# Where the stacked weights are made, when groups are rounded, and where tile 0's first layer stands in a routed mixture-of-experts kernel

## The chip, the cores and the metric

The kernel runs on one core of a Trainium2 chip, as one program from the inputs to the output. The metric is the device time in microseconds (us). Beside it stands one profiled execution, whose trace has every instruction of the five engines (TensorE or PE, with its weight loads as PEld; VectorE or DVE; ScalarE or ACT; GpSimd or POOL; SyncE or SP, which issues most transfers) with start, length and what ended the idle time before it.

## The reference

Three stages stand one behind the other. `x` is 4 sequences of 5,696 tokens of 128 numbers, so N = 22,784 tokens.

```
y  = irfft(rfft(x, 2S) * rfft(h, 2S))[:S]          # a long convolution, per channel
# soft experts: 8 experts of 4 slots each, D = 128, F = 1024
logits = y @ phi                                   # N x 32
slots  = softmax over tokens(logits).T @ y         # 32 x 128
out_s  = relu(slots @ w1[e]) @ w2[e]               # per expert e
z  = softmax over slots(logits) @ out_s            # N x 128
# routed experts: one of 8 per token
gate = z @ w_gate + modality_bias[modality_id]     # N x 8
e    = argmax(gate);  g = softmax(gate)[e]
out  = g * (relu(z @ v1[e]) @ v2[e])               # v1, v2: moe2_w1, moe2_w2
```

Each token's z is a weighted sum of 32 slot outputs. So the kernel never forms z: a token is carried as its 32 softmax weights, and `out_s` is multiplied into the experts' first layer once, which gives a stacked weight of 32 rows per expert. The same is done with the gate's weights.

## The kernel before

**Up to the slots** the program convolves by Fourier transforms on TensorE, makes the slot logits, the softmax weights and the slots' inputs, and loads the slot experts' weights. `prefetch` (line 1528) then issues four loads of the routed experts' first layer, two experts each, into the tile `mw` (called A in the trace). `slot_experts` computes the slots' outputs `oT`. All of this is untouched.

**The part that the change touches first** is written out by hand in `build` (lines 1569 to 1639): on each engine the instructions run in the order in which the program text issues them.

- `gate_weights` multiplies the slots' outputs with the gate's weights. `gate(i)` (function `gate_logits`) makes the logits of the i-th quarter of the tokens: matmuls `gl`, a ScalarE copy (L743, L746), transposes `psl`, and later `add` on VectorE (L764), which adds the modality's bias `bf`. `base` fills `bf` with the first modality's bias, `other` overwrites it where a token has the second (L541). `warm(n)` issues n matmuls whose result nobody reads.
- `push(eh, hf)` calls `expert_stack`: four experts (`eh` is 0 or 1) and half of their columns (`hf`). TensorE multiplies `oT` with `mw` (L781, tile e), ScalarE rounds the product (L782), and the returned function, called later through `seconds(i)`, makes the remainder on VectorE (L785). With the second half of a group of four experts it also issues eight stores of the stacked weights into DRAM (`s_w`, L790).
- `ro.choose` picks the expert of each token of the first part (26 groups of 128 tokens): VectorE's maximum, difference and comparison, ScalarE's exponential (L888), and a one-hot matrix (L894) that is written over the memory of the logits. `ro.offsets` counts tokens per expert with two matmuls (`pre`) and a chain of small VectorE instructions; `ro.gates`, `ro.positions` and `ro.masks` follow.
- `ro.prep(n)` prepares n pairs of groups for sorting: VectorE forms m (L1008), a one-hot of positions (L1010) and token numbers (L1012); then `hi` rounds m on ScalarE (L1016) and `lo` makes the remainder on VectorE (L1019). `prep_all` runs all three. `ro.sort(n, put)` sorts a pair by matmuls `srt` (L1035), copies it on ScalarE (L1037) and scatters it with an indirect transfer from POOL into DRAM (`s_rec`, L1153).
- `ro.table` makes the table of tiles: which expert and which rows of `s_rec` a tile of 256 tokens has. SP reads its entries (`entry`).

**The routed experts** (`routed_experts`) go over 89 tiles. For tile k, `load_w` loads the expert's weights in up to two transfers, `load_rec` the sorted records, `tokT` transposes them (tile pst), `l1(k, h)` makes half h of the first layer (matmuls L1302; ScalarE's rounded relu L1304; VectorE's remainder L1305), `l2` the second layer, `out1` and `out2` the output, `store` scatters it. In between, the rest of the tokens is routed: `late` is a list of small steps (choice, offsets, preparation, tables of the later parts), `run_late(n)` does n of them, and `spend(us)` does as many as a written-down cost allows. `run(k0, k1)` writes out the order; before the loop over tiles it has a prologue, which the change touches. A tile's records may be loaded once the groups of its chunk are scattered: tile 0 needs 9 pairs of groups, tiles 1 and 2 need 11, tile 3 needs 13. Nine pairs are sorted in `build`, four more in the prologue.

Of the kernel before, what the change touches and what calls it, by code (L numbers as in the profile page):

```python
# [53 lines left out]
W3 = 5  # L54
W4 = 8
W5 = 2
W6 = 3
W7 = 10
YBUF = 16
FAR = 1 << 20  # L60
# [1127 lines left out]
def routed_experts(nc, tc, R, P, out, ro, tabs, put):  # L1188

    ident = P["ident"]  # L1190
    with tc.tile_pool(name="p6", bufs=1, reuse_waits="tile") as sp, tc.tile_pool(name="p6p", bufs=1, space=PS, reuse_waits="tile") as pp:
# [155 lines left out]
        def run(k0, k1):  # L1347
# [7 lines left out]
            go(load_rec, k0)  # L1355
            go(load_w, k0, second_layer)
            if k0 == 0:
                for _ in range(2):
                    prep_all(2)
                    ro.sort(2, put)  # L1360
                run_late(7)
            go(entry, k0 + 1)
            go(load_w, k0 + 1, first_layer)
            go(entry, k0 + 2)
# [1 line left out]
            go(load_rec, k0 + 2)  # L1366
            go(load_w, k0 + 1, second_layer)
            go(load_w, k0 + 2, first_layer)
            go(load_rec, k0 + 3)
            go(load_w, k0 + 2, second_layer)  # L1370
            go(tokT, k0)
            go(l1, k0, 0)
            go(l1, k0, 1)
            if k0 == 0:
                spend(PRE)
            go(tokT, k0 + 1)
            for k in range(k0, k1):
# [79 lines left out]
def build(nc, tc, I, O, dbg=None):  # L1457
# [13 lines left out]
    with tc.tile_pool(name="const", bufs=1) as cp:  # L1471
# [98 lines left out]
        with tc.manual_schedule():  # L1570
            base, other = fill
            g = 4 * PIECES[0][1]
            base(bf, 0, g)
            other(bf, 0, g)
            nc.gpsimd.memset(pad, 0.0)
            nc.sync.dma_start(R["rec"][SPARE * TM:].rearrange("(p j) c -> p (j c)", p=128), pad)
            ro = Routing(nc, P, rt, rq, rc, slices(a2, 10 * F), pp, c, l2, pat, ex, v, tabs)
            ro.number()
            put = scatters(nc, tc, R, ro)
            nc.gpsimd.tensor_copy(P["identr"], P["ident"])  # L1580

            def gate(i, between=None):
                return gate_logits(nc, xr, pp, P, cT, bd, bf, l2, i, between)
            def stack(eh, hf):
                return expert_stack(nc, pp, R, oT, mw, mh2, ml2, eh, hf)

            def warm(n):
                keep_warm(nc, pp, P["ones"], n, tag="l", bufs=2)
            stacks, adds = [], []

            def push(eh, hf):
                stacks.append(stack(eh, hf))

            def seconds(*i):

                for i in i:
                    stacks[i]()
                    yield us(512)

            def sums(*i):  # L1600

                for i in i:
                    adds[i]()
                    yield us(400)

            warm(W5)
            gate_weights(nc, pp, oT, wg, bd)
            warm(W5)
            base(bf, g, NG)
            add = gate(0, lambda: warm(W6))  # L1610
            other(bf, g, NG)
            add()
            adds.append(gate(1))
            choose = ro.choose(PARTS[0])
            run_all(itertools.islice(choose, 4))
            push(0, 0)
            run_all(choose)
            offsets = ro.offsets(PARTS[0])
            next(offsets)
            push(0, 1)  # L1620
            push(1, 0)
            run_all(offsets, ro.gates(*PARTS[0][:2]), ro.positions(*PARTS[0][:2]), ro.masks(*PARTS[0][:2]))
            ro.prep_all(1)
            run_all(seconds(0))
            ro.sort(1, put)
            ro.prep_all(2)
            run_all(seconds(1))
            push(1, 1)
            ro.sort(2, put)
            for i in range(3):  # L1630
                ro.prep_all(2)
                if i == 1:
                    run_all(seconds(2, 3))
                ro.sort(2, put)
            run_all(ro.table(tabs[0], CP[1]))
            run_all(sums(0))
            adds.append(gate(2))
            adds.append(gate(3))
            run_all(sums(1, 2))
        if dbg:  # L1640
            nc.sync.dma_start(O["l2"], l2)
            nc.sync.dma_start(O["tab"], tabs[2])
# [30 lines left out]
```

## Time and profile before

| | us |
|---|---|
| three runs | 984.76, 980.85, 983.04 |
| their median | 983.04 |
| the profiled execution | 979.97 |
| its span, first to last instruction | 977.9 |

Shares of the span in which an engine was busy: TensorE 91%, its weight loads 83%, VectorE 71%, ScalarE 62%, POOL 52%. The mean granted TensorE clock was 0.969 of 2.4 GHz.

How to read the profile: a row of the timeline has the start and length of an instruction (or of several merged ones, x4), its engine, line and operation, what it writes and reads, and in brackets how long the engine had been idle before it and what ended that. A product of two fp32 matrices shows as two matmul instructions. A transfer's row on SP is its issue, not its landing.

### The profile page before, as it was taken

The page shows a single profiled execution, that of the slowest core. Times are in us where ns is not written, and L with a number is a line of the kernel's source. Part 1 is how long each engine was busy: PE and PEld are TensorE (multiplying, and loading weights), DVE is VectorE, ACT ScalarE, POOL GpSimd, SP SyncE. Part 2 cuts the span into 40 slices and gives each one's busy share as a digit, 9 for nine tenths or more (in the row PEclk, how much of TensorE's full clock was granted, in tenths as well). Part 3 has the DMA queues.
Part 4 walks back from the last instruction along what each step waited for, and adds up shares of the span by engine and source line. Part 5 has one row for each costly group of instructions (what it writes and reads, how often), then busy time and mean ns, then how long its engine had stood idle before and what let it go on. Part 6 is the DMA issues. An engine that isn't in the chain of part 4 may idle for free. (4 is left out here: it accounts for less than half of the span.)

```text
span 977.9 us, 22643 instructions
## 1 busy us (share of the span) xinstructions
PE 894.0 (91%) x7552; PEld 814.6 (83%) x7552; DVE 695.1 (71%) x1451; ACT 603.2 (62%) x1104; POOL 513.0 (52%) x619
## 2 busy tenths in 40 slices
PE   7999999999999999899845689989999999999996
PEld 7898888878888899788514689979999998999995
DVE  1658687777777555893486779979889987775553
ACT  2655585674765656752233467767777777776673
POOL 2215756738657825381231266656657666665443
PEclk9999999999999999999956899999999999999998
DMA  9915857748559866899966222222223323322221
GB/s 137 329 48 145 264 158 221 239 148 256 191 170 284 327 231 206 331 407 382 303 169 217 73 60 74 75 62 72 71 69 78 76 76 82 75 73 69 59 64 39
DMA packets 147396, 156.66 MB, mean 160 GB/s; under 512 B 71341, under 2 KB 124493, under 8 KB 145210
## 3 DMA queue, kind: packets, MB, share of 16 engines
q1 hardware_dynamic: 137306, 137.43, 47.5%
q0 software_dynamic: 9968, 17.71, 5.6%
q8 instruction: 63, 1.03, 0.5%
q14 instruction: 59, 0.48, 0.2%
HBM read 227.40 MB, written 63.70 MB: 298 GB/s over the span
## 5 line engine op out<-in xcount | busy, mean ns | idle before, releaser
L1305 DVE SCALAR_TENSOR_TENSOR hl<-ph,hh 128x1024 fp32r<-128x1024 f32 x178 | 217.3, 1222 | 92.8 <-ACT hh L1304 91.5
L1342 POOL DMA_INDIRECT out<-y,ids x178 | 180.6, 1015 | 104.4 <-ACT y L1330 54.8
L1304 ACT ACTIVATE hh<-ph 128x1024 fp32r<-128x1024 f32 x178 | 182.7, 1027 | 57.4 <-PE ph L1302 50.1
L1317 PE MATMUL acc<-hh,w 128*128 128x256 f32 x712 | 214.9, 302 | 0.0
L1318 PE MATMUL acc<-hl,w 128*128 128x256 f32 x712 | 201.3, 283 | 0.0
L1319 PE MATMUL acc<-hh,w 128*128 128x256 f32 x712 | 201.3, 283 | 0.0
L1318 PEld LDWEIGHTS acc<-hl,w 128*128 128x128 f32 x712 | 136.5, 192 | 0.0
L1319 PEld LDWEIGHTS acc<-hh,w 128*128 128x128 f32 x712 | 136.1, 191 | 0.0
L1317 PEld LDWEIGHTS acc<-hh,w 128*128 128x128 f32 x712 | 135.9, 191 | 0.0
L1153 POOL DMA_INDIRECT s_rec<-so,dst x80 | 76.9, 962 | 97.4 <-ACT so L1037 85.8
L205 PEld LDWEIGHTS psx<-G,A 128*128 128x128 f32 x890 | 111.7, 196 | 19.1 <-DVE V L217 11.7
L205 PE MATMUL psx<-G,A 128*128 128x128 f32 x890 | 121.6, 284 | 2.5 <-DVE A L140 1.3
L130 PE MATMUL psa<-fw,xs 128*128 128x180 f32 x640 | 110.0, 325 | 11.2 <-POOL xs L169 5.0
L1302 PE MATMUL ph<-x,w 128*128 128x256 f32 x712 | 116.2, 286 | 4.1 <-DVE hl L1305 3.2
L130 PEld LDWEIGHTS psa<-fw,xs 128*128 128x128 f32 x640 | 99.5, 198 | 23.2 <-POOL xs L169 12.6
L140 DVE COPY A<-psa 64x360 f32<-64x360 f32 x160 | 88.5, 553 | 31.6 <-PE psa L130 28.0
L134 ACT COPY A<-psa 64x360 f32<-64x360 f32 x160 | 84.1, 526 | 37.4 <-PE psa L130 34.4
L1302 PEld LDWEIGHTS ph<-x,w 128*128 128x128 f32 x712 | 98.7, 193 | 5.0 <-issue 4.0
L218 POOL TENSOR_TENSOR Y<-Y,V 128x256 f32<-128x256 f32 (+1 forms) x92 | 66.4, 722 | 58.3 <-DVE V L217 49.8
L169 POOL COPY xs<-xr 89x512 f32<-89x512 f32 x68 | 45.7, 674 | 89.6 <-PE psa L130 73.1
L229 ACT COPY yt<-psy 128x512 f32<-128x512 f32 (+1 forms) x92 | 52.7, 572 | 64.9 <-PE psy L102 40.5
L216 DVE TENSOR_TENSOR Y<-psx,H 128x512 f32<-128x512 f32 (+1 forms) x92 | 61.9, 673 | 35.4 <-PE psx L205 32.0
(245 smaller groups left out, 1525.4 us busy)
## 6 DMA issues: line engine op xcount, KB each, us to landing
w<-s_w SPq DMA_DIRECT2D x86, 1536.0 KB
s_yt<-yt SPq DMA_DIRECT2D x88, 256.0 KB
xr<-x SPq DMA_DIRECT2D x16, 640.0 KB
xr<-s_yt SPq DMA_DIRECT2D x18, 512.0 KB
s_w<-ws SPq DMA_DIRECT2D x32, 256.0 KB
L<-s_yt SPq DMA_DIRECT2D x16, 512.0 KB
rt<-s_rec SPq DMA_DIRECT2D x89, 66.0 KB
rt<-s_rec SPq DMA_DIRECT2D x89, 64.0 KB
```

The lines of the kernel that those rows point to most:

```text
L130: nc.tensor.matmul(ps[:, i, :4 * NPAIR], x, fw1, start=True, stop=True)
L134: i = nc.scalar.copy(o, v)
L140: i = nc.vector.tensor_copy(o, v)
L205: nc.tensor.matmul(ps[:, m, :], A[:, 2 * i + m // 2, :, m % 2], G[:, 4 * i + m, :], start=True, stop=True)
L1153: d = nc.gpsimd.indirect_dma_start(rows, bass.IndirectOffsetOnAxis(ap=ro.dst[:LANES, i:i + 1], axis=0), o, None, bounds_check=SPARE * TB - ...
L1302: nc.tensor.matmul(ps[:, TM * j:TM * j + TM], w[k % 3][:, f:f + 128], x[k], start=True, stop=True)
L1304: nc.scalar.activation(o, ps, AF.Relu)
L1305: nc.vector.scalar_tensor_tensor(hl[:, 4 * h:4 * h + 4].rearrange("p j t -> p (j t)"), ps, 0.0, o.bitcast(F32), op0=ALU.max, op1=ALU.subtract)
L1317: nc.tensor.matmul(acc[k], wh, hh[:, f], start=(f == 0), stop=False)
L1318: nc.tensor.matmul(acc[k], wh, hl[:, f], start=False, stop=False)
L1319: nc.tensor.matmul(acc[k], wl, hh[:, f], start=False, stop=(f == 7))
L1342: i = nc.gpsimd.indirect_dma_start(out, bass.IndirectOffsetOnAxis(ap=d[:, j:j + 1], axis=0), y[:, j, :], None, bounds_check=NT - 1, oob_is ...
```

## The change

Three moves, all of them in the order of issue. The work itself stays the same, but for five warm-up matmuls that are dropped.

1. In `build`, `push` for all four (eh, hf) is issued around the first two quarters' logits: two ahead of `gate(0)`, the third between the matmuls and the copy of `gate(0)`, the fourth behind `gate(1)`. The remainders (`seconds`, now `low`) follow early as well: two ahead of the first `add`, the third behind the choice, the fourth in the first preparation; with them go the stores. `base` for the later tokens now stands behind the first two products, `other` for them behind the table.
2. In the five preparations of `build`, `hi` of the next groups is issued ahead of `ro.sort` of the groups before, and `lo` behind it.
3. In the prologue of `run`, tile 0's `tokT` and `l1` stand behind the first two sorted pairs instead of behind all four; the second preparation and sort, the load of tile 3's records, and the seven late steps follow behind them.

```diff
@@ run, the prologue
             if k0 == 0:
-                for _ in range(2):
-                    prep_all(2)
-                    ro.sort(2, put)
-                run_late(7)
+                prep_all(2)
+                ro.sort(2, put)
             go(entry, k0 + 1)
             go(load_w, k0 + 1, first_layer)
...
             go(load_w, k0 + 2, first_layer)
-            go(load_rec, k0 + 3)
-            go(load_w, k0 + 2, second_layer)
             go(tokT, k0)
             go(l1, k0, 0)
             go(l1, k0, 1)
             if k0 == 0:
+                prep_all(2)
+                ro.sort(2, put)
+            go(load_rec, k0 + 3)
+            go(load_w, k0 + 2, second_layer)
+            if k0 == 0:
+                run_late(7)
                 spend(PRE)
             go(tokT, k0 + 1)
@@ build
-            def push(eh, hf):
-                stacks.append(stack(eh, hf))
-
-            def seconds(*i):
-
+            def push(*which):
+                for w in which:
+                    stacks.append(stack(*w))
+
+            def low(*i):
                 for i in i:
                     stacks[i]()
-                    yield us(512)
...
+            first, cols = PARTS[0], PARTS[0][:2]
             warm(W5)
             gate_weights(nc, pp, oT, wg, bd)
-            warm(W5)
+            push((0, 0), (0, 1))
             base(bf, g, NG)
-            add = gate(0, lambda: warm(W6))
-            other(bf, g, NG)
+            add = gate(0, lambda: push((1, 0)))
+            low(0, 1)
             add()
             adds.append(gate(1))
-            choose = ro.choose(PARTS[0])
-            run_all(itertools.islice(choose, 4))
-            push(0, 0)
-            run_all(choose)
-            offsets = ro.offsets(PARTS[0])
-            next(offsets)
-            push(0, 1)
-            push(1, 0)
-            run_all(offsets, ro.gates(*PARTS[0][:2]), ro.positions(*PARTS[0][:2]), ro.masks(*PARTS[0][:2]))
-            ro.prep_all(1)
-            run_all(seconds(0))
-            ro.sort(1, put)
-            ro.prep_all(2)
-            run_all(seconds(1))
-            push(1, 1)
-            ro.sort(2, put)
-            for i in range(3):
-                ro.prep_all(2)
-                if i == 1:
-                    run_all(seconds(2, 3))
-                ro.sort(2, put)
+            push((1, 1))
+            run_all(ro.choose(first))
+            offsets = ro.offsets(first)
+            low(2)
+            run_all(offsets, ro.gates(*cols), ro.positions(*cols), ro.masks(*cols))
+            todo = 0
+            for i, n in enumerate((1, 2, 2, 2, 2)):
+                hi, lo = ro.prep(n)
+                hi()
+                if todo:
+                    ro.sort(todo, put)
+                lo()
+                if i == 0:
+                    low(3)
+                todo = n
+            ro.sort(todo, put)
             run_all(ro.table(tabs[0], CP[1]))
-            run_all(sums(0))
+            other(bf, g, NG)
+            sums(0)
             adds.append(gate(2))
             adds.append(gate(3))
-            run_all(sums(1, 2))
+            sums(1, 2)
```

## Rows read from the trace of the kernel before

**Rows 1.** The page, part 2: busy tenths in 40 slices of the span.

```profile
PE   7999999999999999899845689989999999999996
```

**Rows 2.** Busy time by stretch: engines in order, then granted clock, DMA share, GB/s.

```profile
493.50:514.00 20.50, 9.84 (x38) 4.32 (x38) 16.04 (x52) 6.56 (x15) 9.07 (x9) 0.50 0.73 191
517.40:534.50 17.10, 8.96 (x39) 7.03 (x38) 11.65 (x29) 5.57 (x11) 3.74 (x4) 0.50 0.67 204
```

**Rows 3.** The same view in short stretches, for the DMA share.

```profile
485.50:486.00 0.50, 0.50 (x4) 0.38 (x3) 0.00 (x0) 0.00 (x0) 0.00 (x0) 0.50 0.59 213
...
487.00:487.50 0.50, 0.26 (x4) 0.00 (x0) 0.47 (x2) 0.16 (x1) 0.00 (x0) 1.00 0.06 23
```

**Rows 4.** Timeline of SP, 470 to 520 us: issues of transfers.

```profile
470.89 3.45 SPq L1530 DMA_DIRECT2D A<-moe_w  x4
...
491.28 22.27 SPq L790 DMA_DIRECT2D s_w<-G  x16
...
519.05 0.55 SPq L1267 DMA_DIRECT2D rt<-s_rec  x1
```

**Rows 5.** Timeline of all engines around the first logits and one later product.

```profile
484.33 0.37 ACT L743 COPY xr<-gl 96x256 f32<-96x256 f32 x1 [11.22 <-PE gl L738]
...
485.64 0.58 PE L102 MATMUL psl<-ident,xr 128*128 128x128 f32 x2
...
486.26 0.46 DVE L764 TENSOR_TENSOR xr<-psl,xr 128x192 f32<-128x192 f32 x2 [1.65 <-PE psl L102]
...
488.34 1.06 PE L781 MATMUL e<-A,oT 128*32 128x512 f32 x8
488.45 0.38 DVE L894 TENSOR_TENSOR xr<-small,vm 128x208 bf16<-128x208 f32 x1
...
489.65 0.27 DVE L932 TENSOR_SCALAR ti<-pre 128x104 int32<-128x104 f32 x1 [0.58 <-PE pre L922]
...
497.98 1.93 PE L781 MATMUL e<-A,oT 128*32 128x512 f32 x8
```

**Rows 6.** Groups by line and form, 478.5 to 518 us: busy, mean ns, idle before.

```profile
L1019 DVE TENSOR_TENSOR hl<-A,hl 128x512 fp32r<-128x512 f32 x4 | 2.8, 693 | 2.1 <-ACT hl L1016 2.1
...
L785 DVE TENSOR_TENSOR G<-e,G 128x512 fp32r<-128x512 f32 x4 | 2.6, 684 | 0.0
...
L782 ACT CAST G<-e 128x512 fp32r<-128x512 f32 x4 | 2.3, 586 | 3.2 <-PE e L781 3.2
...
L541 DVE COPY_PREDICATED xr<-A 128x1200 f32<-128x1200 int32 x1 | 1.5, 1504 | 0.0
...
L764 DVE TENSOR_TENSOR xr<-psl,xr 128x512 f32<-128x512 f32 x1 | 0.7, 692 | 2.2 <-PE psl L102 2.2
```

**Rows 7.** Timeline of all engines from tile 0's preparation to tile 3's transposes.

```profile
519.55 0.69 DVE L1019 TENSOR_TENSOR hl<-m,hl 128x512 fp32r<-128x512 f32 x1 [0.27 <-ACT hl L1016]
...
521.58 0.71 PE L1035 MATMUL srt<-hl,oh 128*72 128x264 f32 x2 [0.51 <-ACT so L1037]
...
523.26 0.69 DVE L1019 TENSOR_TENSOR hl<-m,hl 128x512 fp32r<-128x512 f32 x1 [1.95 <-ACT hl L1016]
...
526.98 2.08 PE L1302 MATMUL ph<-x,w 128*128 128x256 f32 x8 [0.87 <-ACT x L1287]
527.21 0.24 DVE L897 TENSOR_TENSOR s<-xr 128x152 bf16<-128x152 bf16 x1
...
529.29 2.36 DVE L1305 SCALAR_TENSOR_TENSOR hl<-ph,hh 128x1024 fp32r<-128x1024 f32 x2 [1.84 <-ACT hh L1304]
...
531.16 0.47 PE L102 MATMUL pst<-identr,rt 128*128 128x128 f32 x2 [1.83 <-DMA rt<-s_rec]
...
531.63 0.31 DVE L932 TENSOR_SCALAR ti<-pre 128x152 int32<-128x152 f32 x1
...
538.82 2.33 DVE L1305 SCALAR_TENSOR_TENSOR hl<-ph,hh 128x1024 fp32r<-128x1024 f32 x2
...
543.16 0.41 PE L102 MATMUL pst<-identr,rt 128*128 128x128 f32 x2
```

More of the change, by code (lines that the diff above doesn't have):

```diff
@@ L56 @@
 W5 = 2
-W6 = 3
 W7 = 10
@@ L1603, in sums @@
                     adds[i]()
-                    yield us(400)
+            first, cols = PARTS[0], PARTS[0][:2]
             warm(W5)
             gate_weights(nc, pp, oT, wg, bd)
-            warm(W5)
+            push((0, 0), (0, 1))
             base(bf, g, NG)
-            add = gate(0, lambda: warm(W6))
-            other(bf, g, NG)
+            add = gate(0, lambda: push((1, 0)))
+            low(0, 1)
             add()
             adds.append(gate(1))
-            choose = ro.choose(PARTS[0])
-            run_all(itertools.islice(choose, 4))
-            push(0, 0)
-            run_all(choose)
-            offsets = ro.offsets(PARTS[0])
-            next(offsets)
-            push(0, 1)
-            push(1, 0)
-            run_all(offsets, ro.gates(*PARTS[0][:2]), ro.positions(*PARTS[0][:2]), ro.masks(*PARTS[0][:2]))
-            ro.prep_all(1)
-            run_all(seconds(0))
-            ro.sort(1, put)
-            ro.prep_all(2)
-            run_all(seconds(1))
-            push(1, 1)
-            ro.sort(2, put)
-            for i in range(3):
-                ro.prep_all(2)
-                if i == 1:
-                    run_all(seconds(2, 3))
-                ro.sort(2, put)
+            push((1, 1))
[14 more added lines that the diff above has]
+            ro.sort(todo, put)
             run_all(ro.table(tabs[0], CP[1]))
-            run_all(sums(0))
+            other(bf, g, NG)
+            sums(0)
             adds.append(gate(2))
             adds.append(gate(3))
-            run_all(sums(1, 2))
+            sums(1, 2)
         if dbg:
```

## The prediction

> **What bounds the kernel now.** I read the page first, part 2, to find the stage. TensorE is busy in nine tenths of nearly every slice, except in slices 20 to 24 of 40 [rows 1], 464 to 587 us, where the program turns from the slot experts to the routed ones. The diff touches only this stretch. Outside it TensorE sets the pace, so a delay or a gain made inside it is kept to the end. Then I read the timeline of the stretch engine by engine, and for each instruction what its engine waited for.
>
> From 486.3 us on VectorE is the chain. It adds the bias to the first gate logits at 486.26, and goes through choice, offsets and positions, five batches of preparation, and the table of tile entries. In the batches it waits only for ScalarE's rounding [rows 5, 6]. Then tile 0 follows: VectorE's second halves of layer 1 at 529.29 and 538.82 stand in one row with the last preparations and the next part's choice and offsets [rows 7]. TensorE waits for it there, not the reverse. So I count what each edit does to VectorE's row, and what holds VectorE up.
>
> **Part 1: stacked weights ahead of the logits.** Four products (eight matmul instructions each, "push"), each with a ScalarE copy and a VectorE remainder, move from among the routing steps to the front. Five warm-up matmuls leave.
>
> *The third product waits for a load.* It reads experts 4 to 7 of the routed first layer. Those four loads of 1 MB are issued by SP from 470.89 to 474.34 [rows 4]. They are the last large thing on the DMA queues: the engines are still 0.59 busy at 485.5 to 486, and a remainder of one engine in sixteen (share 0.06) ends about 487.5 [rows 3]. The before-kernel never notices, since its first product starts at 488.34 [rows 5]. The new one puts this product between the first logits' matmuls and their ScalarE copy. TensorE's matmuls keep their order and ScalarE its own, so both the transposes of the logits and the copy in front of them stand behind this load. The first half (experts 0 to 3, so products one and two) lands earlier, I estimate at half of the remaining way, 482 to 483, and is hidden behind the wait for the second.
>
> Working from 487.6: product 1.06 [rows 5] to 488.65; its copy 0.59 [rows 6] to 489.3; the logits' copies, 0.37 and a shorter second one, together 0.65, to 489.95; two transposes 0.58 to 490.55; the add at 490.65 instead of 486.26 [rows 5]. That is **+4.4**. If the tail of one engine is not there the load ends about 486.4: +3.2.
>
> *The exponential waits for the fourth product.* That product is issued before the choice, and its ScalarE copy stands ahead of the exponential in ScalarE's order. The one-hot of the choice (L894) overwrites the logits that the exponential reads, so it must wait for it. Before, the add began at 486.26 and L894 at 488.45, 2.2 later. Before, a product could start 2.1 after the logits' transposes ended at 486.22 (488.34) [rows 5], and the same holds now: 490.55 + 2.1 + 1.06 + 0.07 + 0.59 + 0.4 for the exponential (as L894 itself) gives 494.75, where VectorE was ready at 490.65 + 2.2 = 492.85. **+1.9.**
>
> *The remainders.* VectorE's four remainders cost 0.68 each [rows 6]. Two now run while VectorE waits for the first logits (free). The third runs while it waits for the offsets' sums, a wait that was 0.58 at 489.65 [rows 5]: +0.15 net. The fourth stays in the row. So three of four leave the batches: 3 x 0.68 = **-2.0**, of which +0.15 comes back.
>
> *The bias of the other modality* (L541, 1.5) moves behind the table. VectorE waits there 2.2 us for the transposes of the third logits [rows 6], and 1.5 fit into that. Nothing, or +1.5 if that cover went. The stores leave SP's row at 491.28 to 513.55 [rows 4] some 5 us earlier. VectorE does not wait for SP there, so I count no gain; the upper bound is in the rivals.
>
> **Part 2: rounding ahead of copies.** In the four batches of two groups VectorE waited 2.1 us in all for ScalarE's rounding, which stood behind copies of sorted rows [rows 6]. The rounding itself must still follow VectorE's first product, some 0.2 a batch: **-1.3**, with -0.9 and -1.7 as bounds.
>
> Parts 1 and 2: 4.4 + 1.9 + 0.15 - 2.0 - 1.3 = **+3.1**.
>
> **Part 3: tile 0's first layer ahead of the last sorts.** VectorE ends its first batch at 520.24 [rows 7]. Before, it went on with the second batch and the choice to 527.45, of which 1.95 was a wait, so 5.3 of work. Then came tile 0's two halves, ending at 531.65. Now the halves come first. Tile 0's records are issued by 519.6 [rows 4] and TensorE is free after the second sort at 522.3. Transposes and copy take about 1.0 (from the second sort; 525.5 to 527.0 before, with an exponential between), so layer 1 starts about 523.3 instead of 526.98. VectorE's first half follows 2.3 later (526.98 to 529.29) and the second ends 4.7 after the start [rows 7]: 528.0. Until 525.6 VectorE is idle, 5.3 us. Then the second batch and the choice, 5.3 + 0.3 for their own rounding, to 533.6; the offsets' matmuls and the wait for them, no longer covered by the halves, 0.4; offsets at 533.95 instead of 531.63. **+2.3.** Tile 1's transposes stand on TensorE behind the offsets' matmuls, which need the choice. They start near 534.1 instead of 531.16 where they waited for records, and layer 2 of tile 0 goes with them. What follows is VectorE's row again, so the halves of tile 1 (538.82) come 2.3 later. SP's order is unchanged, but POOL's last two scatters come some 7 us later and SP's fourth records load waits for them. Tile 3 uses these at 543.16 [rows 7], which leaves time. Bounds: +1.0 if the layer's matmuls ran at 2.4 GHz (they took 2.08 at the lower level, 1.2 GHz: 0.50 was granted from 517.4 to 534.5 [rows 2, 7]), and +3.2 if tile 0's records land a microsecond after the second sort.
>
> **Sum.** 3.1 + 2.3 = +5.4 on the profiled execution: 979.97 to 985.4 (span 977.9 to 983.3). The median of the three runs, 983.04, lies 3.1 above that execution, so I expect **988.4**. Bounds of the parts: the low ends (3.2 for 4.4, 1.0 for 2.3, 1.7 for 1.3) give +2.5, 985.5; the high ends (0.9 for 1.3, 3.2 for 2.3, and the low clock below) give +9, 992.
>
> **The clock.** A product took 1.06 at the full level and 1.93 at the lower one, at 497.98, in a stretch granted 0.50 [rows 2, 5]. The new order lets TensorE stand still for part of the time up to 487.6, so the two products on the chain and the transposes could run low: 2 x 0.87, and about 0.6 for logits and transposes, +2.3. The Trainium skill, "TensorE: Matmul & The Clock Gate", section "HAM oscillation — how this bites in real kernels", says that idle gaps between bursts throttle the array again; by that rule the sum would be +7.7, against +5.4 by the level that the before-kernel had at this moment. The trace bears it out in part: 0.50 after the idle time behind 493.5, but 1.06 for a product at 488.34 after a stretch with idle gaps.
>
> **Rivals.**
> *Low clock at the gates* (chance 0.11): +7.7, 990.7. The stretch behind 493.5 speaks for it, the level at 488.34 against it.
> *One of the two costs isn't there* (0.36): either the load lands in time or ScalarE's order costs little (parts 1 and 2 come out near 0, leaving +2.3), or part 3 is hidden (leaving +3.1), or some of the delay is taken up in the slices after 540, where TensorE is not yet full [rows 1]. 983 to 987, about 985.5. For it: the sums are of small terms. Against: VectorE's row has little slack.
> *Faster, the stores' queue was the bound* (0.13): SP was busy with the stores up to 513.55 [rows 4], and only then took up tile 0's loads. If loads and scatters come earlier, TensorE's wait of 1.83 for tile 1's records [rows 7] goes and about 1 us at tile 0. With the 3.3 of parts 1 and 2 kept whole that is -6, 977. It decides if the second half of the experts' weights has landed by 484.3, when the first logits' matmuls ended, and if tile 0's records come so early that VectorE need not stand idle before its halves. Rows 3 speak against the first, the order of SP's loads behind the logits' matmuls against the second.
>
> **How the numbers follow.** The forecast has 0.40 (own range 986.5 to 990.5). A change of 0.5% (4.9 us) is about what a measurement of this kernel can tell from no change, since its three runs span 980.85 to 984.76. Faster than 978.1: the third rival, 0.13. Slower than 987.95: about 0.33 of the forecast's 0.40 and all of the low clock's 0.11: 0.44. The rest, 0.43, is within. The range leaves out the faster rival and a little of the top: 981.5 to 992.
>
> **What the profile of the changed kernel would show.** Right: the third product's matmuls start at 486.4 to 488 behind a DMA wait, with the logits' add at 489.5 to 492; L894 waits 1.5 to 3 us for the exponential; no wait over 0.3 for rounding in the five batches, with one remainder among them instead of four; VectorE idle about 5 us before tile 0's first half; offsets of the next part 13 to 14 us after the end of tile 0's first batch, not 11.4. Wrong: an add before 488 (load in time), an L894 without a wait, tile 1's transposes no later than before relative to that batch, or a TensorE so slow or so full after 540 that the shift isn't seen at 600.

## The result, and the profile after

Six runs gave a median of 993.04 us (990.49 to 996.19), beside 982.18 for the kernel before in the same comparison: a ratio of **1.0114** (95% interval 1.0080 to 1.0147), some 11 us slower. Forecast were 988.4, with a range up to 992.0: the direction was right, the size half of what was measured, and the time lies above the range. Two later comparisons of the same kernel gave 1.0086 (1.0043 to 1.0129) and 1.0086 (1.0068 to 1.0103). In two of the later comparisons (marked * in the table below) the loop over tiles took 60 to 70 us longer in every kernel, that of before with them (1047 and 1049 us), for a reason that stays open, so ratios and the steps of the changed stretch are compared and not times. The profiled execution took 992.85 us, with a span of 990.7.

The page of the changed kernel, part 2 (the first line answers to [rows 1]; the second is the granted TensorE clock in tenths):

```profile
PE   7999999999999999899844779989999999999996
...
PEclk8999999999999999999955899999999999999998
```

Again it is slices 20 to 24 in which TensorE is not full, with about as much in them as before (8, 4, 4, 7, 7 tenths, and 8, 4, 5, 6, 8 before), and in slices 21 and 22 the mean clock is near one half. The view by stretch gives it exactly (engines, then clock, DMA share, GB/s). Before, full clock came back between the two stretches of [rows 2]; here it stays at 1.2 GHz (0.50) for 58 us:

```profile
485.50:492.00 6.50, 4.17 (x36) 1.20 (x36) 2.54 (x8) 2.26 (x3) 1.25 (x6) 1.00 0.99 332
492.00:519.00 27.00, 11.22 (x41) 4.17 (x41) 17.42 (x56) 7.24 (x18) 4.39 (x5) 0.50 0.57 147
519.00:530.00 11.00, 7.21 (x31) 2.95 (x31) 6.04 (x23) 2.10 (x6) 5.26 (x5) 0.50 0.20 50
530.00:550.10 20.10, 10.16 (x43) 8.51 (x44) 12.77 (x35) 6.49 (x12) 3.74 (x4) 0.50 0.63 209
```

Then the timeline around the first logits, which answers to [rows 5] (lines are one less than before). The work ahead of the change ended 4.2 us later in this execution, so distances count, not times of day.

```profile
488.83 1.05 PE L780 MATMUL e<-A,oT 128*32 128x512 f32 x4 [0.22 <-DMA A<-moe_w]
...
492.04 1.92 PE L780 MATMUL e<-A,oT 128*32 128x512 f32 x4 [2.16 <-DMA A<-moe_w]
...
494.07 0.59 ACT L781 CAST G<-e 128x512 fp32r<-128x512 f32 x1 [4.16 <-PE e L780]
494.55 0.37 ACT L742 COPY xr<-gl 96x256 f32<-96x256 f32 x1
...
495.25 0.64 PE L101 MATMUL psl<-ident,xr 128*128 128x128 f32 x2 [1.28 <-ACT xr L745]
...
495.92 0.46 DVE L763 TENSOR_TENSOR xr<-psl,xr 128x192 f32<-128x192 f32 x2 [6.37 <-PE psl L101]
...
498.75 1.94 PE L780 MATMUL e<-A,oT 128*32 128x512 f32 x8
...
501.23 0.38 ACT L887 ACTIVATE xr<-xr 128x208 f32<-128x208 f32 x1
501.64 0.38 DVE L893 TENSOR_TENSOR xr<-small,vm 128x208 bf16<-128x208 f32 x1 [3.65 <-ACT xr L887]
```

The reader is to see the two forecast waits in their places: the third product stands behind a DMA for 2.16 us, with ScalarE's copies and VectorE's add (6.37 idle) behind it; and the one-hot L893 waits 3.65 us for the exponential, which stands behind the fourth product. Both products are long: 1.92 for the second half of the third, which is two experts and takes 1.05 at full clock (in after_third, below), and 1.94 for the fourth, where 1.06 was counted for a product.

The groups of the five batches, [rows 6] (busy, mean ns, idle before): VectorE's wait for rounding is 1.2 instead of 2.1, where 0.8 was forecast.

```profile
L1018 DVE TENSOR_TENSOR hl<-A,hl 128x512 fp32r<-128x512 f32 x4 | 2.8, 693 | 1.2 <-ACT hl L1015 1.2
```

Timeline from the third logits to tile 1's halves, [rows 7]:

```profile
526.28 1.50 PE L737 MATMUL gl<-G,bd 128*32 128x384 f32 x8
526.38 0.69 DVE L763 TENSOR_TENSOR xr<-psl,xr 128x512 f32<-128x512 f32 x1 [1.10 <-PE psl L101]
...
529.48 0.46 DVE L763 TENSOR_TENSOR xr<-psl,xr 128x288 f32<-128x288 f32 x1 [2.41 <-PE psl L101]
529.94 0.68 DVE L1007 TENSOR_TENSOR m<-c,gm 128x512 f32<-128x512 f32 x1
...
531.31 0.69 DVE L1018 TENSOR_TENSOR hl<-m,hl 128x512 fp32r<-128x512 f32 x1 [0.22 <-ACT hl L1015]
...
537.11 2.35 DVE L1304 SCALAR_TENSOR_TENSOR hl<-ph,hh 128x1024 fp32r<-128x1024 f32 x2 [5.11 <-ACT hh L1303]
...
545.54 0.32 DVE L931 TENSOR_SCALAR ti<-pre 128x152 int32<-128x152 f32 x1 [0.53 <-PE pre L921]
...
552.73 2.33 DVE L1304 SCALAR_TENSOR_TENSOR hl<-ph,hh 128x1024 fp32r<-128x1024 f32 x2
```

VectorE stands idle 5.11 us ahead of tile 0's halves, as forecast. Before that, between the table and tile 0's preparation, it waits 2.41 us for the third logits' last matmuls, which take 1.50, and their transposes.

### The profile page after: what moved, and what is told of

It reads as the page before. It is cut to its first block, busy times and chain, and to the rows that moved or that the text cites. A ratio compares the mean times of both kernels' runs of the same rounds, so it can differ in the third digit from the quotient of the medians.

```text
span 990.7 us, 22623 instructions
## 1 busy us (share of the span) xinstructions
PE 895.8 (90%) x7542; PEld 813.7 (82%) x7542; DVE 695.9 (70%) x1451; ACT 602.5 (61%) x1104; POOL 514.4 (52%) x619
## 5 line engine op out<-in xcount | busy, mean ns | idle before, releaser
L129 PEld LDWEIGHTS psa<-fw,xs 128*128 128x128 f32 x640 | 100.3, 200 | 24.1 <-POOL xs L168 13.5
```

The lines of the kernel that those rows point to most:

```text
L129: nc.tensor.matmul(ps[:, i, :4 * NPAIR], x, fw1, start=True, stop=True)
```

## The experiments

All kernels are told apart by the same steps of VectorE's row, from first start to first start: from the last copy of the slots' outputs to the first logits' add; to the one-hot; from the first preparation to the table ("batches"); to tile 0's preparation; to tile 1's first remainder ("prologue"). The part left out, from the one-hot to the first preparation, holds 7.2 to 7.5, and 7.8 and 7.9 in p3_choice_first and fourth_late. "Sum" is the whole way from the slots' outputs to tile 1. Times are ratios to the kernel before in the same comparison.

| kernel | add | one-hot | batches | tile 0 | prologue | sum | ratio (95%) |
|---|---|---|---|---|---|---|---|
| before | 5.27 | 2.18 | 12.87 | 9.34 | 20.70 | 57.83 | 1 |
| before_again | 5.30 | 2.19 | 12.87 | 9.37 | 20.69 | 57.83 | 0.9975 (0.9954–0.9996) |
| the change | 10.75 | 5.73 | 10.10 | 10.81 | 22.79 | 67.57 | 1.0114 (1.0080–1.0147) |
| after_again* | 9.24 | 3.85 | 10.21 | 10.81 | 22.80 | 64.28 | 1.0086 (1.0043–1.0129) |
| after_third | 9.38 | 5.72 | 10.06 | 10.81 | 22.78 | 66.14 | 1.0086 (1.0068–1.0103) |
| p1_only* | 10.77 | 4.57 | 12.57 | 10.72 | 20.69 | 66.71 | 1.0087 (1.0046–1.0128) |
| p2_only* | 5.30 | 2.19 | 11.72 | 10.82 | 20.65 | 58.02 | 0.9983 (0.9940–1.0027) |
| p3_only* | 4.07 | 2.19 | 12.87 | 9.35 | 23.50 | 59.20 | 1.0077 (1.0038–1.0116) |
| p3_again* | 4.08 | 2.19 | 12.87 | 10.72 | 22.84 | 59.93 | 1.0029 (0.9991–1.0068) |
| fourth_late* | 9.48 | 2.19 | 10.14 | 11.05 | 22.80 | 63.55 | 1.0042 (0.9999–1.0086) |
| third_late* | 7.14 | 5.29 | 10.15 | 10.81 | 22.77 | 63.55 | one run |
| both_late | 7.50 | 2.18 | 10.71 | 10.81 | 22.80 | 61.22 | 1.0010 (0.9981–1.0039) |
| best_no3 | 6.94 | 2.19 | 10.71 | 10.81 | 20.64 | 58.59 | 0.9994 (0.9977–1.0010) |
| no_load | 9.35 | 3.85 | 10.15 | 10.81 | 22.80 | 64.33 | 1.0040 (1.0018–1.0063) |
| no_load_warm | 8.21 | 3.85 | 10.10 | 9.46 | 22.79 | 61.79 | 1.0069 (1.0040–1.0097) |
| warm_wait | 12.15 | 3.85 | 10.06 | 10.81 | 23.18 | 67.43 | 1.0050 (1.0019–1.0082) |
| warm_five | 9.34 | 3.85 | 10.09 | 10.81 | 22.79 | 64.25 | 1.0069 (1.0046–1.0092) |
| p3_choice_first | 4.57 | 2.26 | 12.87 | 10.72 | 19.96 | 58.15 | 0.9978 (0.9948–1.0007) |
| best | 5.72 | 2.19 | 10.62 | 10.81 | 19.91 | 56.56 | 0.9982 (0.9961–1.0002) |
| best_warm* | 8.94 | 2.19 | 10.65 | 12.49 | 19.90 | 61.48 | 1.0008 (0.9974–1.0042) |

The kernel before against itself came out at 0.9975, with an interval that leaves out 1. So ratios closer than about 0.3% say nothing here, and the intervals are somewhat too narrow.

### The parts alone

**p1_only** is the change with the old loop over batches and the old prologue; **p2_only** and **p3_only** are the kernel before with one part:

```diff
 p2_only            # seconds(0) to seconds(3) and push(1, 1) stay in the loop
-            ro.prep_all(1)
-            run_all(seconds(0))
-            ro.sort(1, put)
...
+            for i, n in enumerate((1, 2, 2, 2, 2)):
+                hi, lo = ro.prep(n)
+                hi()
+                if todo:
+                    ro.sort(todo, put)
+                lo()
...
 p3_only            # only the hunk of run(), as in the change
```

> The changed order of the stacked weights alone; the preparations and the prologue are those of the kernel before. Theory A (waits in program order): the logits' add comes 5.5 us later, counted from the copies of the slots' outputs, the one-hot 3.5 us later still, three remainders leave the batches (-1.7), so 6 to 8 us slower than before. Theory B (the moves on the engines are small, and what cost the time is TensorE's clock, which stood at half from 492 to 550 in the changed kernel): if the clock drops as there, the same 6 to 8 us, if it keeps the levels of before, under 5 us. Theory C (the prologue is the main cost): under 3 us.

> The rounding ahead of the copies alone. Theory A: the waits for rounding in the batches shrink from 2.1 us to about 0.9, so 1.0 to 1.5 us faster, which is less than a run's scatter. Theory B: the same. Theory C: no change.

> Tile 0's first layer ahead of the last two sorts alone. Theory A: VectorE idle about 5 us before tile 0's first remainder, offsets of the next part 2.1 us later, counted from tile 0's first preparation; 2 us slower. Theory B: about 1 us, if TensorE's clock is not low there. Theory C: over 5 us slower.

Part 1 alone costs what the whole change costs. It also shortened the batches by only 0.3, not by 2.0. Its group says why:

```profile
L1018 DVE TENSOR_TENSOR hl<-A,hl 128x512 fp32r<-128x512 f32 x4 | 2.8, 693 | 3.7 <-ACT hl L1015 3.7
```

With the remainders gone from the row, the wait for rounding behind the copies grew from 2.1 to 3.7. Part 2 alone gives 1.15, both together 2.7: the remainders had been filling part of that wait. Part 3 cost 2.8 in this profile and 0.77% in time, more than its steps explain, so it was run again.

> The changed prologue alone, a second time, since the first time the trace's stretch of tile 0 was 2.8 us longer and the whole 8 us. Theory A: 2 to 3 us slower, 0.2 to 0.3%, as the stretch says. Theory D (later scatters cost more in the loop over tiles): 0.5% or more slower, and the time from tile 2's first remainder to the end longer than the 436 us of before.

The same kernel then cost 2.1 in its prologue, as in the change, and 0.29% in time. The two intervals overlap, and a cost in the loop over tiles does not show: behind tile 2's first remainder the two profiles took 496 and 501 us, the others marked * 500 to 510. So the first figure is most likely scatter. The step to tile 0 also came out otherwise, 10.72 after 9.35.

### Where the products stand

**fourth_late** puts the fourth product behind the offsets' matmuls, **third_late** the third behind the logits' copies and transposes, **both_late** both behind the offsets' matmuls.

```diff
 fourth_late
-            push((1, 1))
             run_all(ro.choose(first))
             offsets = ro.offsets(first)
+            next(offsets)
+            push((1, 1))
 third_late
-            add = gate(0, lambda: push((1, 0)))
+            add = gate(0)
+            push((1, 0))
 both_late          # as fourth_late, and
-            add = gate(0, lambda: push((1, 0)))
+            add = gate(0)
+            push((1, 0), (1, 1))     # in place of push((1, 1)) and low(2)
...
-                    low(3)
+                    low(2, 3)
```

> The changed kernel, with the fourth product behind the choice and the offsets' matmuls instead of ahead of the choice. Theory A: the one-hot no longer waits for the exponential (3.65 us in the changed kernel), the logits' add stays late; 3 to 4 us faster than the changed kernel, so 5 to 8 us slower than before. Theory B: the clock stays low, and under 2 us come back. Theory C: nothing comes back.

> The changed kernel, with the third product behind the first logits' copies and transposes; the fourth stays ahead of the choice. Theory A: the logits' add comes 5 to 7 us after the copies of the slots' outputs instead of 10.75, but the load's wait comes back at the one-hot, which waits for the exponential behind both products: 7 to 9 us from add to one-hot instead of 5.7, so at most 2 to 3 us are gained. Theory B: the gain of 5 us at the add is kept.

> The changed kernel with the third and the fourth product behind the offsets' matmuls; the first two products, the rounding ahead of copies and the prologue stay. Theory A: the logits' add comes 5 to 5.5 us after the copies of the slots' outputs (10.75 in the changed kernel, 5.27 before), the one-hot 2.2 later, two remainders are left in the batches; 7 to 9 us faster than the changed kernel, so within 2 us of the kernel before. Theory B: the clock still falls behind the first logits and 4 us or more stay. Theory C (the stores' place on SP matters): like the changed kernel.

Each moved product gave its own wait back: 2.19 at the one-hot with the fourth behind, 7.1 at the add with the third behind. In third_late the delay only moved on, since the second logits' copy then stood behind the third product (one-hot 5.29). With both behind, the time is that of before within the interval, though the steps still hold 3.4 more. So most of the cost lies in the two waits.

But the add stayed at 5.7 to 7.5 without any third product ahead of it (best, best_no3, both_late), and the load's own share was still open. no_load leaves out the weights of experts 4 to 7 and reads those of 0 to 3 twice:

```diff
 no_load
-        nc.tensor.matmul(ps[...], ..., mw[:, 4 * eh + em, sl], ...)
+        nc.tensor.matmul(ps[...], ..., mw[:, em, sl], ...)
 no_load_warm       # no_load, and ahead of the third product
+                warm(5)
 best_no3           # both_late with the prologue of before
```

> The change, but the third and fourth products read the weights of experts 0 to 3 instead of 4 to 7 (the stacked weights of experts 4 to 7, and with them part of the output, are not the reference's): nothing waits for the late load any more, while the products stand where the change puts them. Theory (the load is over half of the cost at the add): the add falls from 9.2 to 10.8 to about 7.0 us after the slots' outputs, which leaves +1.7 for the third product and its copy ahead of the logits' copies; the one-hot's step stays at 3.8, since the fourth product still stands ahead of the exponential; time 2 to 4 us below the change. Rival (the position in the queues is the whole cost and the load is hidden): the add stays above 9 and the time stays that of the change.

> no_load (the third and fourth products read the weights of experts 0 to 3, so the stacked weights of experts 4 to 7 are not the reference's) with five warm-ups ahead of the third product. In no_load the first half of the load came 1.3 us late and the clock was low from 484.3 to 487.7, so its add at 9.35 mixed three causes. Theory (the late load is half or more of the cost at the add): with neither the load nor a low clock the add comes 7.0 to 8.0 us after the slots' outputs, the warm-ups' 1.2 included, and the one-hot's step is 3.85; 62 to 63 to tile 1's first remainder; a time 0.2 to 0.5% above before. Rival (the place in TensorE's and ScalarE's queues is the whole cost): the add stays at 9 or above and the time at 0.7% or more above.

> The change without its prologue and with the third and fourth product behind the offsets' matmuls, so that no product of the second load and no copy of the fourth stands ahead of the logits or the exponential: what parts 1 and 2 give without their two waits. Theory: the add 4.1 to 5.7 (7.5 if the clock is low), the one-hot's step 2.18, the batches 2.2 shorter than before, the step to tile 0 at 10.8 where the clock is low there, before's 11.17, 2.34 and 7.19 behind: -0.5 to -2 us from before, a time 0.05 to 0.2% less. Rival (the reordering has a cost of its own, in clock or in the queues): as much as both_late, 0.1% above or more.

In no_load the first half of the load was late itself (a wait of 1.31 in the first product) and the clock low from 484.3 to 487.7, so the 9.35 as such decides nothing. The rows behind `base` do: that copy stands on ScalarE ahead of the third product's, and the clock is full there, in after_third up to the logits' transposes. Timelines of ScalarE and the add, first of after_third, then of no_load:

```profile
484.52 1.19 ACT L536 COPY xr<-A 128x1200 f32<-128x1200 f32 x1
488.32 0.59 ACT L781 CAST G<-e 128x512 fp32r<-128x512 f32 x1 [2.60 <-PE e L780]
...
489.96 0.45 DVE L763 TENSOR_TENSOR xr<-psl,xr 128x192 f32<-128x192 f32 x2 [4.61 <-PE psl L101]
```

```profile
487.80 1.19 ACT L536 COPY xr<-A 128x1200 f32<-128x1200 f32 x1
488.93 0.59 ACT L781 CAST G<-e 128x512 fp32r<-128x512 f32 x1
...
490.56 0.46 DVE L763 TENSOR_TENSOR xr<-psl,xr 128x192 f32<-128x192 f32 x2 [1.93 <-PE psl L101]
```

With the load ScalarE stands idle for 2.60 us behind `base`, and the add comes 4.25 behind the end of `base`. Without it nothing is idle there, and the add comes 1.57 behind. best_no3, which has no third product there, has 1.04 (rows below). So the load is worth 2.7 at the add, and the third product with its copy 0.5. That is over half of the cost at the add, as the theory of no_load says, though the add itself did not fall to 7.0.

no_load_warm against warm_five (below) is the same pair with five warm-ups in the wait and the clock full in both. Timelines, first of warm_five, then of no_load_warm:

```profile
487.73 1.05 PE L780 MATMUL e<-A,oT 128*32 128x512 f32 x4 [0.46 <-DMA A<-moe_w]
...
490.50 0.46 DVE L763 TENSOR_TENSOR xr<-psl,xr 128x192 f32<-128x192 f32 x2 [4.60 <-PE psl L101]
...
492.32 1.06 PE L780 MATMUL e<-A,oT 128*32 128x512 f32 x8
...
494.35 0.38 DVE L893 TENSOR_TENSOR xr<-small,vm 128x208 bf16<-128x208 f32 x1 [1.76 <-ACT xr L887]
```

```profile
489.13 1.07 PE L780 MATMUL e<-A,oT 128*32 128x512 f32 x8
...
491.95 0.46 DVE L763 TENSOR_TENSOR xr<-psl,xr 128x192 f32<-128x192 f32 x2 [3.13 <-PE psl L101]
```

Here the difference is only 9.34 - 8.21 = 1.1. The warm-ups delay the third product by 1.3 where there is no load to wait for, and fill part of the wait where there is one. And in no_load_warm the first half of the load came 0.3 later: the first logits' matmuls start 2.72 behind the slots' outputs, in warm_five 2.38. So 1.1 is what the load costs on top of the warm-ups, not its price in the change.

The first two products cost something too once no load stands behind them. In best, where the first half came in time and the clock was full, the add stands at 5.72. The order of before takes 4.07 there at full clock (p3_only, p3_again); its own 5.3 holds a stretch at half [rows 3]. That is 1.65 more. In best_no3, third_late and both_late the first product waited 0.85, 1.05 and 1.42 us for the first half, and the add came at 6.94, 7.14 and 7.50. The timeline of best_no3 shows through what:

```profile
483.36 0.58 ACT L781 CAST G<-e 128x512 fp32r<-128x512 f32 x1 [0.22 <-PE e L780]
483.84 1.19 ACT L536 COPY xr<-A 128x1200 f32<-128x1200 f32 x1
484.93 0.37 ACT L742 COPY xr<-gl 96x256 f32<-96x256 f32 x1
...
486.07 0.46 DVE L763 TENSOR_TENSOR xr<-psl,xr 128x192 f32<-128x192 f32 x2 [1.41 <-PE psl L101]
```

`base` for the later tokens, a ScalarE copy of 1.19, moved behind the first two products. There it stands between their copies and that of the logits. Before, ScalarE was idle for 11.22 ahead of the logits' copy [rows 5]. In the change these 1.65 do not come on top: ScalarE was through with `base` 2.60 before the third product was there. In time no_load_warm and warm_five do not differ (1.0069 both), and no_load is 0.3% below, so the load's share rests on the steps alone. best_no3 shows parts 1 and 2 without both waits: no gain that can be measured.

### The clock

```diff
 warm_wait
+            def third():
+                warm(12)
+                push((1, 0))
+                warm(4)
-            add = gate(0, lambda: push((1, 0)))
+            add = gate(0, third)
 warm_five          # the same with warm(5), and none behind
```

> The changed kernel with 12 warm-up matmuls ahead of the third product and 4 behind it, so that TensorE works while it waits for the load. Theory A (waits in program order; the clock adds to them): the third and fourth product take 1.06 each instead of 1.92, the transposes and second logits less too, so the one-hot comes 2 to 3 us earlier than in the changed kernel, counted from the copies of the slots' outputs; the wait for the load itself stays. Theory B (the clock is the whole cause): 6 us or more come back and the time is that of before. Theory C (the warm-ups run at half clock and outlast the load): no gain, or 1 us worse.

> The change with its five dropped warm-ups put back ahead of the third product (1.2 us by 12 of them taking 2.94). Theory (the clock falls in the waits for the load, and it falls when TensorE stands still): the clock stays up to the fourth product, the third and fourth take 1.06, the add comes about 9.2 after the slots' outputs and the one-hot's step is 3.85; time as the change or 1 to 3 us less. Rival (five are too few to matter): a low clock at the third product again in this profile, with steps near 10.7 and 5.7.

> The kernel before, profiled a second time: how much of the stretch is scatter. Theory: the step from the table to tile 0's preparation was 9.34 in the first profile only because the clock was up at that moment, and comes out at 10.7 to 10.8 here, so that 1.4 of the +9.7 found in the change's profile is no part of the change; from the slots' outputs to tile 1's first remainder 57.8 to 59.3. Rival: the step belongs to the order of before and stays at 9.3; then the change costs these 1.4. Time: ratio 1.000 within its interval.

> The changed kernel a second time, beside the others. Theory A: 0.9 to 1.2% slower; the steps that depend on matmuls of the stacked weights vary with TensorE's clock by up to 3 us, the others repeat within 0.1 us. Theory B (the long stretch at half clock is a habit of this kernel): the clock is at half from about 10 us after the slots' outputs to tile 1 again. Theory C: under 0.5%.

> The change, profiled a third time. The first profile had its clock fall while the third product waited (steps 10.75 to the add, 5.73 to the one-hot), the second after the fourth product (9.24 and 3.85). Theory: the step to the add scatters between 9.2 and 10.8 and the step to the one-hot between 3.8 and 5.8, according to where the clock falls; from the slots' outputs to tile 1's first remainder 64 to 68, which is 5 to 9 above before, and a time 0.8 to 1.1% above. Rival: the low clock at the gates was the exception, so 64 to 65 and a time of 0.5 to 0.7% above.

With warm-ups in the wait, the products took 1.06 to 1.07 and the one-hot's wait fell to 1.76, as in the row of warm_five above: what the forecast had (1.9). In warm_wait the 12 warm-ups took 2.94 us and outlasted the load, and the add came later still; five gave the same one-hot and left the add where it was (9.34). Without them the clock fell at 492.0 in the first profile, where the third product had waited; in after_third with the first logits' transposes, ahead of the fourth product; and in after_again only when that was done (one-hot 5.73, 5.72, 3.85). Timeline of after_third, the second half of the third product at full and the fourth at half clock:

```profile
487.16 1.05 PE L780 MATMUL e<-A,oT 128*32 128x512 f32 x4 [1.46 <-DMA A<-moe_w]
...
492.79 1.94 PE L780 MATMUL e<-A,oT 128*32 128x512 f32 x8
```

before_again was to show that the step of 9.34 to tile 0 had been luck. That theory fell: it came again, 9.37, and in none of the changed kernel's three profiles. In the windows and the timeline of before_again full clock returns for 3.4 us just there, and the third logits' matmuls take 0.85, not the 1.50 of the change:

```profile
495.30:515.80 20.50, 9.81 (x38) 4.33 (x38) 16.02 (x52) 6.54 (x15) 9.12 (x9) 0.50 0.74 191
515.80:519.20 3.40, 1.80 (x16) 0.83 (x15) 0.69 (x1) 1.32 (x3) 0.00 (x0) 1.00 0.54 180
```

```profile
517.23 0.85 PE L738 MATMUL gl<-G,bd 128*32 128x384 f32 x8
...
519.54 0.46 DVE L764 TENSOR_TENSOR xr<-psl,xr 128x288 f32<-128x288 f32 x1 [1.52 <-PE psl L102]
520.00 0.68 DVE L1008 TENSOR_TENSOR m<-c,gm 128x512 f32<-128x512 f32 x1
```

The step follows the clock and not the order as such: p3_again, with the order of before up to there, had 10.72, and no_load_warm, with the new one, 9.46. In p3_again, the same kernel as p3_only (9.35), the clock did not return (view by stretch, then timeline):

```profile
496.60:537.40 40.80, 21.07 (x85) 11.90 (x86) 24.94 (x68) 13.34 (x29) 12.87 (x13) 0.50 0.68 199
```

```profile
515.86 1.50 PE L738 MATMUL gl<-G,bd 128*32 128x384 f32 x8
```

This also settles the rival that the copy `other` (1.5), which now stands behind the table, makes the step longer: with it the step takes 10.81 at half and 9.46 at full clock, without it 10.72 and 9.35.

### Another order of the prologue

**p3_choice_first** is the kernel before with the second preparation and the choice still ahead of tile 0's layer and only the second sort behind it; **best** is both_late with that prologue; **best_warm** adds three warm-ups behind each sort of the batches and six behind the last. The lines of p3_choice_first are shown against the prologue of the change.

```diff
 p3_choice_first
                 prep_all(2)
                 ro.sort(2, put)
+                prep_all(2)
+                run_late(7)
             ...
             go(l1, k0, 1)
             if k0 == 0:
-                prep_all(2)
                 ro.sort(2, put)
             ...
-                run_late(7)
                 spend(PRE)
```

> The kernel before with another prologue: tile 0's first layer stands ahead of the last two sorts on TensorE, but the second preparation and the choice stay ahead of tile 0's remainders on VectorE. Theory A: VectorE has work while tile 0's layer runs, the wait of 1.84 before tile 0's first remainder goes; 0.5 to 2 us faster than before, and 3 to 4 us faster than with the prologue of the changed kernel. Theory B: no difference from the prologue alone. Theory C: slower than before by 2 us or more, since the last scatters come later.

> Third and fourth product late, rounding ahead of copies, and the prologue with the choice ahead of tile 0's remainders. Theory A: two remainders out of the batches (-1.3), less waiting for rounding (-1.3), the prologue (-1.4): 3 to 4 us faster than before, 0.3 to 0.4%. Theory B and C: no faster than before.

> The best version with warm-up matmuls behind the sorts of the five batches (three each) and behind the last one (six), where TensorE stands idle. Theory A and B (the clock): the level stays up through the table, and the time from the table to tile 0's first preparation is 9.4 us instead of 10.8; tile 0's matmuls too run at the full level: 2 to 3 us faster than the best version, 0.4 to 0.6% faster than before. Theory C: no difference to the best version.

With VectorE's own work ahead, the idle time before tile 0's halves is 1.26 in the timeline of p3_choice_first, where the change has 5.11 and before 1.84, and the prologue is 0.7 shorter than before, where the change made it 2.1 longer:

```profile
525.05 2.08 PE L1302 MATMUL ph<-x,w 128*128 128x256 f32 x8 [2.94 <-ACT x L1287]
...
527.37 2.36 DVE L1305 SCALAR_TENSOR_TENSOR hl<-ph,hh 128x1024 fp32r<-128x1024 f32 x2 [1.26 <-ACT hh L1304]
```

best is 1.3 us shorter than before in its steps. In time it can't be told from before (0.9982, upper end 1.0002), and it beats the change. best_warm had full clock behind the table for a while and still lost 1.7 there: VectorE's copy of the table and ScalarE's of the logits stood 3.23 and 4.49 us in a wait for which the profile names no instruction, 2.6 and 3.2 us beyond the end of the matmuls that they read. What it was stays open; the kernel is not better than best.

## Why the prediction was half right

Against before (57.83 in two profiles) the change's three profiles are 9.7, 6.5 and 8.3 longer, 8.2 in the mean, and the ratios say 8.4 to 11 us. Forecast was 5.4. Behind the stretch nothing came back, as predicted: from tile 2's first remainder to the end it took 434.8 and 433.3 in the two comparisons without *, before 435.9 and 434.6.

- **The third product, +4.4:** measured +5.5, +4.0 and +4.1. Size, place and path were right: it started its second half 6.9, 6.5 and 6.6 behind the slots' outputs, where 6.6 was assumed, and the first two products are hidden behind that wait. What the sum did not see is that these products, with `base`, cost 1.65 by themselves and the third 0.5, so that without the load (2.7) the add would still come later than before. It was also added to a row that was slow itself: [rows 3] has a granted clock of 0.50 at 485.5 to 486.0, and at full clock the order of before has its add 1.2 earlier.
- **The exponential, +1.9:** measured +1.67 at full clock and +3.5 at half (two of three). The mechanism was right.
- **Remainders and rounding, +0.15 - 2.0 - 1.3 = -3.15:** the batches gave -2.7 and the offsets' step -0.08, in sum right within 0.4. The rounding alone gave -0.9, with one wait of 0.43 where none over 0.3 was forecast. Counted separately they were wrong, since each covers the other.
- **`other`, nothing:** it did hide behind the wait for the third logits, all but 0.1.
- **Part 3, +2.3:** measured +2.1. Idle 5.11 against 5.3; the offsets came 13.5 behind the end of tile 0's first batch (532.00, from 531.31 and 0.69, to 545.54), where 13 to 14 were forecast.
- **"The clock": the step that failed.** The sum took the products, transposes and logits' matmuls at the full level and left the lower one to the rival "Low clock at the gates" with 0.11. Of the missing 2.8 us, 1.47 is the step to tile 0, which the sum did not have at all: full clock did not return there (0.50 granted up to 550.1), and the logits' matmuls and transposes stand on VectorE's path. Another 1.0 is the one-hot's step at half clock, 1.9 more in two profiles of three. The rest, 0.3, is batches that gave less. In the first profile the second half of the third product, 1.92 instead of 1.05, adds 0.9 at the add.

How much of the 1.47 belongs to the change is not shown. Five profiles have the order of before up to the prologue (before, before_again, p3_only, p3_again, p3_choice_first); in three of them full clock came back behind the table, in two it did not. Of the 14 with a changed order, best_warm left out, only no_load_warm had it. Against the mean of those five the change costs 0.9 at this step and 5.1 at the add, and the sum stays as it is.

The argument against that rival was the full clock of a product at 488.34 before [rows 5]. It belonged to an order in which warm-ups stood in that place and nothing waited for a load; the change took away both. In the rival the two products and the transposes run low, which made +7.7. The mean of the three profiles, +8.2, is near it in part by luck, since only about 1.1 of its 2.3 was found at the gates in the mean and the 1.47 had no place in it. The Trainium skill, "TensorE: Matmul & The Clock Gate", section "HAM oscillation — how this bites in real kernels", says that idle gaps between bursts of matmuls lower the clock again. The trace agrees in the first profile, where the fall at 492.0 stands behind 2.16 us of waiting. What warm_five adds: giving the warm-ups back restores the gates (3.85), not the step behind the table (10.81), and 6.4 us of the steps' 8.2 remain; its time of 1.0069 is not to be told from 1.0086.

Of the other rivals, neither came true: both waits and the cost of part 3 were there, and nothing shows that the earlier stores gained time.

Not settled: what decides whether the clock returns behind the table. It did in before twice, in p3_only once of two, and in no_load_warm.

## What to carry to other kernels

Work that is moved ahead "because its inputs are ready" must be followed through every engine that it crosses: here a matmul that waits for a load held up, through two engines' orders, an add that needs neither the product nor the load. Price each moved instruction also at the lower clock if its engine idles in front of it, and take an upper level seen in the old order as evidence for the old order only. Edits that fill or empty the same wait are one term of the sum: here each alone gave 0.3 and 1.15, and both together 2.7.

## What the hardware showed that was not expected

- The stretch at half clock is not the same in two executions of one kernel, and a single profile's step may be off by 1.4 to 1.9 us for that reason (one-hot 3.85 and 5.72; tile 0 9.35 and 10.72). With the same two waits of TensorE ahead (1.46 and 1.28 us) the clock fell behind the second in after_third and held to the end of the fourth product in after_again.
- The first half of the load ended a long wait of the first product in some profiles (1.42 in both_late) and a short one in others (0.19 in fourth_late), so that the time of a landing varied by over a microsecond with the same program ahead of it. The add follows it: it came 3.78 behind the start of the first logits' matmuls in best_no3, third_late and both_late alike, while these started 3.16, 3.36 and 3.73 behind the slots' outputs.
